# Decode layer on one core: w_up in two loads, w_down in blocks of 4, 4 and 5 rows, and a two-row store of the result

## The chip, the core and the metric

The kernel runs on one NeuronCore of a Trainium2 chip. The metric is the device time of one execution in microseconds (us). "Engines" are PE (matmul), PEld (its weight loads), DVE (vector), ACT (scalar), POOL (GpSimd) and SP (sync), which issues nearly all DMA loads here. "DMA engine" is one of the sixteen that move the bytes (the page counts 16, and a load over 128 partitions has 16 completions in the traces). "Landing" is the time of the last completion that a transfer reports.

## The reference, cut to what matters

One token passes through a pre-norm layer: attention over a cache of 32 heads x 4096 positions x 128, then a gated MLP.

```python
h  = x + attention(layernorm(x), k_cache, v_cache, wq, wo)     # x: 1 x 640
g  = layernorm(h) @ w_gate                                     # 640 x 1728
u  = layernorm(h) @ w_up                                       # 640 x 1728
h2 = h + (gelu(g) * u) @ w_down                                # 1728 x 640
```

All is bf16. The weights and caches are 84 MB and each is read once, so the kernel is a stream of loads with arithmetic beside it. The change concerns the last lines: the loads of w_up and w_down, the products with them, and the store of h2.

## The kernel before: the parts that the change touches

The 640 rows of w_gate and w_up lie as 128 partitions x 5 chunks. Of the 1728 rows of w_down, 13 x 128 form row blocks 0 to 12, and the first 64 rows stand apart in wd_lo (blocks 13 and 14). All loads leave from one queue, in program order.

```python
# loads, in queue order (K, V and wo come earlier)
wd_v = B_w_down[192:1728, :].rearrange("(a p r) n -> p a r n", a=3, r=4)
wd_d = wd_sb[:, 0:12, :].rearrange("p (a r) n -> p a r n", a=3)
d_w1 = P.dma("sync", wd_sb[:, 12, :], B_w_down[64:192, :], mults[NG - 1, 1])
for o in (0, 1, 2, 3, 32, 33, 34, 35):          # 4 partitions each, at a step of 4
    lo = o - o % 32
    d_wp = P.dma("sync", wd_lo[o:o + 13:4, :, :], ..., c_wd, chan="wp")
d_wg = P.dma("sync", wg_sb, B_w_gate[:, :].rearrange("(p c) n -> p c n", c=5), pvs[NG - 2])
d_wu = P.dma("sync", wu_sb, B_w_up[:, :].rearrange("(p c) n -> p c n", c=5))
d_wd = [P.dma("sync", wd_d[:, a, lo:hi, :], wd_v[:, a, lo:hi, :])
         for a, lo, hi in ((0, 0, 4), (1, 0, 4), (2, 0, 3), (2, 3, 4))]
# ... cut: wo products, layer norm ...
def glu(ps, w, *ws):        # 5 chunks x 15 columns of output; w's columns 4 apart for 12 of 15, adjacent for 3
    ...
ga = glu(ps_g, wg_sb, hl, d_wg)
up = glu(ps_u, wu_sb, d_wu)
# ... cut: gelu; g9 multiplies by u and writes hm ...
def down(ms, qs=range(4)):  # a product per row block m and quarter q of the 640 columns
    ...                     # quarter q accumulates in PSUM partition 32 * q, 160 columns
T(down([12]), g9, d_w1)
T(down([13, 14]), d_wp)
T(down(range(4)), d_wd[0])
T(down(range(4, 8)), d_wd[1])
T(down(range(8, 11)), d_wd[2])
dn = {q: T(down([11], [q]), d_wd[3]) for q in (0, 2, 1, 3)}
os = [V(lambda e, q=q: e.tensor_copy(out_row[0:1, 160 * q:160 * q + 160], ps_d[32 * q:32 * q + 1, 0:160]), dn[q])
      for q in range(2)]
os += [A(lambda e, q=q: e.copy(out_row[0:1, 160 * q:160 * q + 160], ps_d[32 * q:32 * q + 1, 0:160]), dn[q])
       for q in range(2, 4)]
d_out = P.dma("sync", out[0, :, :], out_row[:, :], *os)
P.op("sync", None, d_out)
```

`P.dma(engine, out, in, waits...)` issues a transfer; `V`, `A`, `T` put an instruction on DVE, ACT or PE with what it waits for.

The softmax here doesn't subtract the row's maximum and nothing guards it: scores larger than these inputs give would overflow.

## Time and profile before

| | before |
|---|---|
| median time | 202.98 us (202.97 to 203.59, 3 runs) |
| span of the profiled execution | 201.9 us |
| DMA | 84.30 MB, 418 GB/s over the span |
| w_up landed, hm started | 194.62, 197.35 us |
| last w_down load landed | 199.31 us |
| last product ends, store issued | 199.95, 200.69 us |
| store: last completion | 201.82 us |

To read it: the DMA engines are full until about 197 us (81% busy from 197.0 to 197.5, 34% in the half microsecond after it), so the last 5 us are the only place where this change can win. The lines themselves are shown in the prediction below. One line that it only tells of is the page's chain, followed back from the end, by line:

```profile
DMA v_slot<-in_A_v_cache_dram 55%; DMA v_slot<-in_B_w_up_dram 13%; PE psum L363 8%; DVE prod L375 7%; PE psum L167 6%; SPq L59 3%; DVE sc L381 2%; PE psum L492 1%; PE psum L514 1%; PE psum L352 1%; DVE out_row L524 0%; DVE hm L507 0%; DVEq L114 0%
```

The reader is to see w_up's load in second place and no w_down load at all.

### The profile page before, as it was taken

Reading aid. Unit: us, or ns where it says so; the run is one execution under the profiler, and the core shown is the slowest. Engines: PE = TensorE matmul, PEld = TensorE weight load, DVE = VectorE, ACT = ScalarE, POOL = GpSimd, SP = SyncE. Lnnn points to the kernel's source line nnn. Section 1 sums busy time; section 2 is a strip of 40 time slices with the busy share of each in tenths; the row PEclk is TensorE's granted clock in tenths of the full one; section 3 lists DMA queues with packets and bytes.
Section 4 is the critical chain, followed back from the end, with each engine's and each line's share of the span. In section 5 each row is a group of like instructions: output and inputs, shape, how many; then the busy total and the mean of one; then the engine's idle time right before and its main releaser. Section 6 shows DMA issues by size and latency. Waiting matters only on the chain.

```text
span 201.9 us, 2002 instructions
## 1 busy us (share of the span) xinstructions
PE 121.4 (60%) x1008; PEld 34.7 (17%) x756; DVE 100.9 (50%) x51; ACT 12.6 (6%) x33; POOL 30.6 (15%) x36
## 2 busy tenths in 40 slices
PE   0108009849408980994379166934990786779665
PEld 0101000001200120112011101020120012279563
DVE  0110197885598039906960993089519914120321
ACT  2010100001000100010000000100100010100101
POOL 6400000000010007101700450026006300100000
PEclk9999999999955698599579755995797599555555
DMA  9999999999999999999999999999999999999991
GB/s 341 422 425 435 429 422 429 416 474 425 429 422 422 422 448 448 435 416 429 422 422 474 422 429 422 429 416 474 429 429 416 429 422 444 402 419 444 428 387 61
DMA packets 3848, 84.30 MB, mean 418 GB/s; under 512 B 450, under 2 KB 772, under 8 KB 1156
## 3 DMA queue, kind: packets, MB, share of 16 engines
q1 hardware_dynamic: 3842, 84.23, 97.6%
q8 instruction: 4, 0.07, 0.1%
q10 hardware_dynamic: 2, 0.00, 0.0%
HBM read 84.23 MB, written 0.00 MB: 417 GB/s over the span
## 4 chain that ended last, share of the span: by engine, by line
DMA 68%; PE 18%; DVE 10%; SPq 3%; issue 1%; DVEq 0%
DMA v_slot<-in_A_v_cache_dram 55%; DMA v_slot<-in_B_w_up_dram 13%; PE psum L363 8%; DVE prod L375 7%; PE psum L167 6%; SPq L59 3%; DVE sc L381 2%; PE psum L492 1%; PE psum L514 1%; PE psum L352 1%; DVE out_row L524 0%; DVE hm L507 0%; DVEq L114 0%
## 5 line engine op out<-in xcount | busy, mean ns | idle before, releaser
L375 DVE TENSOR_TENSOR prod<-k_slot,qb 128x8192 bf16<-128x8192 bf16 x16 | 75.2, 4734 | 7.0 <-DMA k_slot<-in_A_k_cache_dram 5.2
L167 PE MATMUL psum<-prod,id_b 128*128 128x512 bf16 x233 | 65.4, 437 | 0.0
L381 DVE TENSOR_REDUCE sc<-psum 128x128 f32<-128x2048 f32 x8 | 18.3, 2291 | 49.1 <-PE psum L167 49.1
L352 PE MATMUL psum<-prod,id_b 128*128 128x512 bf16 x23 | 10.7, 467 | 50.5 <-DVE prod L375 47.1
L385 POOL TENSOR_TENSOR p_bd<-pt,own 128x512 bf16<-128x512 bf16 x6 | 24.4, 4071 | 89.5 <-ACT pt L382 89.5
L363 PE MATMUL psum<-v_slot,p_bd 128*16 128x512 bf16 x224 | 18.2, 484 | 5.1 <-DMA v_slot<-in_A_v_cache_dram 5.0
L352 PEld LDWEIGHTS psum<-prod,id_b 128*128 128x128 bf16 x23 | 2.3, 100 | 72.4 <-DVE prod L375 50.4
L369 PEld LDWEIGHTS psum<-hs,po_sb 128*128 128x128 f32 x64 | 9.1, 208 | 23.9 <-issue 23.4
L363 PEld LDWEIGHTS psum<-v_slot,p_bd 128*16 128x16 bf16 x224 | 5.8, 105 | 36.0 <-DMA v_slot<-in_A_v_cache_dram 27.9
L369 PE MATMUL psum<-hs,po_sb 128*128 128x4 f32 x64 | 8.5, 256 | 0.1
L392 ACT COPY po_sb<-psum 128x512 f32<-128x512 f32 x7 | 4.1, 586 | 71.8 <-PE psum L363 71.8
L382 ACT ACTIVATE pt<-sc,zero_t 128x128 bf16<-128x128 f32 x8 | 3.2, 401 | 71.2 <-DVE sc L381 71.2
L335 PE MATMUL psum<-arena,xlnB 128*32 128x512 bf16 x20 | 3.3, 627 | 6.2 <-DMA arena<-in_A_wq_dram 6.2
L462 PE MATMUL psum<-aP,arena 128*128 128x1 bf16 x160 | 6.7, 178 | 0.1
L462 PEld LDWEIGHTS psum<-aP,arena 128*128 128x128 bf16 x160 | 6.6, 131 | 0.2 <-DMA arena<-in_A_wo_dram 0.2
L492 PE MATMUL psum<-hlnT,v_slot 128*128 128x1 bf16 x150 | 5.1, 171 | 1.8 <-DMA v_slot<-in_B_w_up_dram 1.8
L389 POOL MEMSET spare<- 1x1 f32 x1 | 0.1, 90 | 36.6 <-DVE p_bd L385 36.6
L492 PEld LDWEIGHTS psum<-hlnT,v_slot 128*128 128x128 bf16 x150 | 5.0, 116 | 2.4 <-DMA v_slot<-in_B_w_up_dram 1.9
L308 PE MATMUL psum<-one_bf,x_row 1*128 1x1 bf16 x5 | 0.4, 177 | 8.3 <-DMA x_row<-in_A_x_dram 8.3
L363 PE MATMUL psum<-k_slot,p_bd 128*16 128x512 bf16 x32 | 3.6, 629 | 2.9 <-DVE p_bd L385 2.9
L340 DVE CAST qb<-psum 128x512 bf16<-128x512 f32 x1 | 0.7, 692 | 9.1 <-PE psum L167 9.1
L311 DVE COPY xx<-psum 128x5 f32<-128x5 f32 x1 | 0.2, 165 | 8.7 <-PE psum L308 8.7
(72 smaller groups left out, 35.1 us busy)
## 6 DMA issues: line engine op xcount, KB each, us to landing
k_slot<-in_A_k_cache_dram SPq DMA_DIRECT2D x8, 4096.0 KB, 25.5
v_slot<-in_A_v_cache_dram SPq DMA_DIRECT2D x7, 4096.0 KB, 16.7
arena<-in_A_wq_dram SPq DMA_DIRECT2D x1, 5120.0 KB, 15.8
arena<-in_A_wo_dram SPq DMA_DIRECT2D x2, 2560.0 KB, 34.5
k_slot<-in_A_v_cache_dram SPq DMA_DIRECT2D x1, 4096.0 KB, 26.1
v_slot<-in_B_w_gate_dram SPq DMA_DIRECT2D x1, 2160.0 KB, 21.3
v_slot<-in_B_w_up_dram SPq DMA_DIRECT2D x1, 2160.0 KB, 25.9
k_slot<-in_B_w_down_dram SPq DMA_DIRECT2D x2, 640.0 KB, 27.6
```

Of the source, the lines that this page charges most:

```text
L59: ev = self.op(eng, lambda e: e.dma_start(out, in_), *deps, dma=True, chan=chan)
L167: built = e.matmul(out, lhsT, rhs, start=start, stop=stop)
L335: mm = held if hf else lambda e, *a, **k: e.matmul(*a, **k)
L352: mm = held if n or not first else lambda e, *a, **k: e.matmul(*a, **k)
L363: i = e.matmul(ps_o[a:a + 16, :], p_bd[:, 4 * b:4 * b + 4, :].rearrange("p g j -> p (g j)"), vt[:, 4 * b:4 * b + 4, :], start=(b < 4), sto ...
L369: i = e.matmul(ps_a[:, bass.ds(at, 4)], po_sb[:, 128 * r:128 * r + 128], hs[:, r, :], start=(r == 0), stop=(r == 3))
L375: mults[G, i] = VM(lambda e: e.tensor_tensor(out=prod[:, i, :, :], in0=kt[:, 64 * i:64 * i + 64, :], in1=qb[:, G, :].unsqueeze(1).to_broad ...
L381: reds[G] = VR(lambda e: e.reduce_sum(sc[:, :], ps_f.rearrange("p (g d) -> p g d", d=16), axis=AX.X), folds[G, 1])
L385: blocks[G] = on(lambda e: e.tensor_tensor(out=p_bd[:, :, :], in0=pt[:, :].unsqueeze(2).to_broadcast([128, 128, 4]), in1=own[:, :].unsquee ...
L392: evs[G] = AS(lambda e: e.copy(po_sb[:, :], ps_o), pvs[G])
L462: r = e.matmul(ps_p[:, c:c + 1], wo_sb[:, i, c::5], aP[:, i:i + 1], start=False, stop=(i == 31), skip_group_check=True)
L492: i = e.matmul(ps[:, m:m + 1], ws, hlnT[:, c:c + 1], start=(c == 0 and m == 0), stop=(c == 4), skip_group_check=True)
```

## The change

The intent: start the products with w_up before all of it is there, keep the wait for w_down short at the end, and empty PSUM with one copy per engine in place of two. The first takes two loads. The second takes the 160 KB of row block 12 out of the front of the queue. For the third, quarters 0 and 1 of PSUM (partitions 0 and 32) are copied by one DVE instruction over 33 partitions, quarters 2 and 3 by one of ACT. The result then lies in partitions 0 and 32 and is stored as two rows. With the new row blocks, 5 of the 15 weight loads per chunk of w_gate and w_up take columns 5 apart, 8 take columns 4 apart and 2 adjacent ones; before, it was 12 at 4 and 3 adjacent.

```diff
-    out_row = sb("out_row", [1, D], BF16)
+    out_row = sb("out_row", [33, 320], BF16)
...
-    d_w1 = P.dma("sync", wd_sb[:, 12, :], B_w_down[64:192, :], mults[NG - 1, 1])
+    blocks_d = ((64, 0, 4), (576, 4, 4), (1088, 8, 5))
+    def down_load(j, lo, hi):    # rows lo to hi of block j, waits for mults[NG - 1, 1]
...
-    d_wu = P.dma("sync", wu_sb, B_w_up[:, :].rearrange("(p c) n -> p c n", c=5))
-    d_wd = [... for a, lo, hi in ((0, 0, 4), (1, 0, 4), (2, 0, 3), (2, 3, 4))]
+    d_wu = [P.dma("sync", wu_sb[:, lo:hi, :], wu_v[:, lo:hi, :]) for lo, hi in ((0, 3), (3, 5))]
+    d_wd = [down_load(0, 0, 4), down_load(1, 0, 4), down_load(2, 0, 4), down_load(2, 4, 5)]
...
+    col = (0, 320, 160, 480)     # first column of each quarter
...
-    up = glu(ps_u, wu_sb, d_wu)
+    glu(ps_u, wu_sb, range(3), d_wu[0])
+    up = glu(ps_u, wu_sb, range(3, 5), d_wu[1])
...
-    T(down([12]), g9, d_w1)
-    T(down([13, 14]), d_wp)
+    T(down([13, 14]), g9, d_wp)
...
-    T(down(range(8, 11)), d_wd[2])
-    dn = {q: T(down([11], [q]), d_wd[3]) for q in (0, 2, 1, 3)}
-    os = [ ... four copies of 1 x 160 ... ]
-    d_out = P.dma("sync", out[0, :, :], out_row[:, :], *os)
+    T(down(range(8, 12)), d_wd[2])
+    dn = [T(down([12], [q]), d_wd[3]) for q in range(4)]
+    os = [V(lambda e: e.tensor_copy(out_row[0:33, 0:160], ps_d[0:33, 0:160]), dn[1]),
+          A(lambda e: e.copy(out_row[0:33, 160:320], ps_d[64:97, 0:160]), dn[3])]
+    d_out = P.dma("sync", out[0, :, :].rearrange("o (q n) -> (o q) n", q=2), out_row[::32, :], *os)
```

(Cuts are marked with "...".)

More of the change, by code (lines that the diff above doesn't have):

```diff
@@ L443, in bass_sequential_preLN__gqa_block_cached__glu_gated_geglu__decode_kernel @@
     wd_sb = k_slot[1][:, 0:15 * D].rearrange("p (m n) -> p m n", m=15)
-    wd_v = B_w_down[192:1728, :].rearrange("(a p r) n -> p a r n", a=3, r=4)
-    wd_d = wd_sb[:, 0:12, :].rearrange("p (a r) n -> p a r n", a=3)
-    d_w1 = P.dma("sync", wd_sb[:, 12, :], B_w_down[64:192, :], mults[NG - 1, 1])
+    blocks_d = ((64, 0, 4), (576, 4, 4), (1088, 8, 5))
+    at_row = {m0 + r: (lo + r, k) for lo, m0, k in blocks_d for r in range(k)}
+    def down_load(j, lo, hi):
+        row, m0, k = blocks_d[j]
+        return P.dma("sync", wd_sb[:, m0 + lo:m0 + hi, :],
+                     B_w_down[row:row + 128 * k, :].rearrange("(p r) n -> p r n", r=k)[:, lo:hi, :], mults[NG - 1, 1])
     for o in (0, 1, 2, 3, 32, 33, 34, 35):
@@ L451, in bass_sequential_preLN__gqa_block_cached__glu_gated_geglu__decode_kernel @@
     d_wg = P.dma("sync", wg_sb, B_w_gate[:, :].rearrange("(p c) n -> p c n", c=5), pvs[NG - 2])
-    d_wu = P.dma("sync", wu_sb, B_w_up[:, :].rearrange("(p c) n -> p c n", c=5))
-    d_wd = [P.dma("sync", wd_d[:, a, lo:hi, :], wd_v[:, a, lo:hi, :])
-             for a, lo, hi in ((0, 0, 4), (1, 0, 4), (2, 0, 3), (2, 3, 4))]
+    wu_v = B_w_up[:, :].rearrange("(p c) n -> p c n", c=5)
+    d_wu = [P.dma("sync", wu_sb[:, lo:hi, :], wu_v[:, lo:hi, :]) for lo, hi in ((0, 3), (3, 5))]
+    d_wd = [down_load(0, 0, 4), down_load(1, 0, 4), down_load(2, 0, 4), down_load(2, 4, 5)]
     T(lambda e: e.matmul(ps_p[:, 0:5], id_f[:, :], xx[:, 0:5], start=True, stop=False, skip_group_check=True), xc, c_idf)
@@ L471, in resid @@
             i = e.matmul(ps_d[32 * q:32 * q + 1, 0:160], ones_f[:, 0:1],
-                         hX[:, 32 * q:32 * q + 32, :].rearrange("p a c -> p (a c)"), start=True, stop=False)
+                         hX[:, col[q] // 5:col[q] // 5 + 32, :].rearrange("p a c -> p (a c)"), start=True, stop=False)
         return i
@@ L479, in bass_sequential_preLN__gqa_block_cached__glu_gated_geglu__decode_kernel, with glu @@
         hlnT[:, :], hT[:, 0:5], ln[:, 0:1], ln[:, 4:5], ALU.subtract, ALU.mult), residual)
-    def glu(ps, w, *ws):
+    def glu(ps, w, cs, *deps):
         def fn(e):
-            for c in range(5):
+            for c in cs:
                 for m in range(15):
-                    if m < 12:
-                        ws = w[:, c, 192 + 512 * (m // 4) + m % 4:192 + 512 * (m // 4) + 512:4]
-                    elif m == 12:
-                        ws = w[:, c, 64:192]
+                    if m < 13:
+                        lo, k = at_row[m]
+                        ws = w[:, c, lo:lo + 127 * k + 1:k]
                     else:
@@ L494, in fn @@
             return i
-        return T(fn, *ws)
-    ga = glu(ps_g, wg_sb, hl, d_wg)
-    up = glu(ps_u, wu_sb, d_wu)
+        return T(fn, *deps)
+    ga = glu(ps_g, wg_sb, range(5), hl, d_wg)
+    glu(ps_u, wu_sb, range(3), d_wu[0])
+    up = glu(ps_u, wu_sb, range(3, 5), d_wu[1])
     g1 = V(lambda e: e.tensor_tensor(out=g_t[:, :], in0=ps_g[:, 0:15], in1=own_g[:, :], op=ALU.mult), ga, c_gm)
@@ L514, in fn @@
                     i = e.matmul(ps_d[32 * q:32 * q + 1, 0:160], hm[0:rows, m:m + 1],
-                                 wd[0:rows, 160 * q:160 * q + 160], start=False, stop=(m == 11))
+                                 wd[0:rows, col[q]:col[q] + 160], start=False, stop=(m == 12))
             return i
         return fn
-    T(down([12]), g9, d_w1)
-    T(down([13, 14]), d_wp)
+    T(down([13, 14]), g9, d_wp)
     T(down(range(4)), d_wd[0])
     T(down(range(4, 8)), d_wd[1])
-    T(down(range(8, 11)), d_wd[2])
-    dn = {q: T(down([11], [q]), d_wd[3]) for q in (0, 2, 1, 3)}
-    os = [V(lambda e, q=q: e.tensor_copy(out_row[0:1, 160 * q:160 * q + 160], ps_d[32 * q:32 * q + 1, 0:160]), dn[q])
-          for q in range(2)]
-    os += [A(lambda e, q=q: e.copy(out_row[0:1, 160 * q:160 * q + 160], ps_d[32 * q:32 * q + 1, 0:160]), dn[q])
-           for q in range(2, 4)]
-    d_out = P.dma("sync", out[0, :, :], out_row[:, :], *os)
+    T(down(range(8, 12)), d_wd[2])
[3 more added lines that the diff above has]
+    d_out = P.dma("sync", out[0, :, :].rearrange("o (q n) -> (o q) n", q=2), out_row[::32, :], *os)
     P.op("sync", None, d_out)
```

## The prediction

> **What bounds the kernel now.** I read the page first (whole span), then the DMA issues, the timeline of the last 20 us, the chain of waits, and last a table of half-microsecond windows over the end. The page's second part shows that nothing but the transfers can bound the bulk of the kernel:
>
> ```profile
> PE   0108009849408980994379166934990786779665
> DMA  9999999999999999999999999999999999999991
> GB/s 341 422 425 435 429 422 429 416 474 425 429 422 422 422 448 448 435 416 429 422 422 474 422 429 422 429 416 474 429 429 416 429 422 444 402 419 444 428 387 61
> ```
>
> The DMA row is 9 in 39 of 40 slices of 5.05 us, and 84.30 MB move at about 420 GB/s. The change moves the same weight bytes, so up to the last slice it can only reorder transfers. What is left to win lies after 191 us, and there these lines of the timeline carry the argument (columns: start, duration, engine, line, operation, count, idle time before it and what ended it):
>
> ```profile
> 187.35 0.17 DVE L468 COPY hT<-psum 128x5 f32<-128x5 f32 x1 [6.93 <-PE psum L462]
> 190.27 2.57 PE L492 MATMUL psum<-hlnT,v_slot 128*128 128x1 bf16 x75
> 194.67 2.58 PE L492 MATMUL psum<-hlnT,v_slot 128*128 128x1 bf16 x75 [1.83 <-DMA v_slot<-in_B_w_up_dram]
> 197.35 0.17 DVE L507 TENSOR_TENSOR hm<-gu,psum 128x15 bf16<-128x15 f32 x1 [2.84 <-PE psum L492]
> 197.58 0.30 PE L514 MATMUL psum<-k_slot,hm 128*1 128x160 bf16 x4 [0.33 <-DVE hm L507]
> 197.81 0.43 PE L514 MATMUL psum<-wd_lo,hm 48*1 48x160 bf16 x8
> 198.18 1.77 PE L514 MATMUL psum<-k_slot,hm 128*1 128x160 bf16 x48
> 199.97 0.66 DVE L524 CAST out_row<-psum 1x160 bf16<-1x160 f32 x2 [2.45 <-PE psum L514]
> 200.01 0.60 ACT L526 CAST out_row<-psum 1x160 bf16<-1x160 f32 x2 [6.20 <-PE psum L514]
> 200.69 0.27 SPq L59 DMA_DIRECT2D out_dram<-out_row  x1
> ```
>
> The reader is to see one serial tail: w_up has landed at 194.62, its 75 products take 2.58 us, hm follows, then 60 products with w_down (4 + 8 + 48), two copies one after the other on each engine, and the store. The chain of waits names the same: w_up's transfer, then L492, L507, L514, L524. Read alone, it promises about 1.5 us for splitting w_up. But the chain shows only the waits that ended last. The next one is hidden just behind it, in the issues of w_down (KB, microseconds from issue to landing, taken in windows around each issue):
>
> ```profile
> 169.15 0.43 SPq L59 DMA_DIRECT2D k_slot<-in_B_w_down_dram  x1
> k_slot<-in_B_w_down_dram SPq DMA_DIRECT2D x1, 640.0 KB, 27.0
> ...
> 169.62 1.59 SPq L59 DMA_DIRECT2D k_slot<-in_B_w_down_dram  x1
> k_slot<-in_B_w_down_dram SPq DMA_DIRECT2D x1, 640.0 KB, 28.1
> ...
> k_slot<-in_B_w_down_dram SPq DMA_DIRECT2D x1, 480.0 KB, 27.7
> k_slot<-in_B_w_down_dram SPq DMA_DIRECT2D x1, 160.0 KB, 27.6
> ```
>
> The four big loads land at 169.15 + 27.0 = 196.2, 169.62 + 28.1 = 197.7, 171.25 + 27.7 = 198.95 and 171.7 + 27.6 = 199.3 us (the third issue begins where the second ends, 169.62 + 1.59 + 0.04; the view of w_down's tile gives 171.7 as the last issue's start). The products of 198.18 to 199.95 never wait, because each block is there a few tenths before its turn. **So w_down's last landing, 199.3, lies only 0.65 us before the end of the last product.** That is the floor under any gain ahead of the products.
>
> [...] the last w_down load's 16 completions spread from 197.28 to 199.31. [...] weight loads of the w_down products come in groups of four every 133 ns. [...] within a row of 15, start to start is 33 ns where the columns are 4 apart, 27 ns where they are adjacent, and 40 ns in the wo products (5 apart). [...]
>
> **The change, part by part.**
>
> 1. *The 160 KB load of row block 12 leaves the front of the queue and becomes part of blocks 0 to 12.* Everything that follows it up to w_up lands earlier by 160 KB / 420 GB/s = 0.39 us: w_gate about 189.1, w_up about 194.2. The gate gains nothing, since it starts at 190.27 on hlnT. The blocks land at 195.8, 197.35, 198.95 (block 2, now 4 rows of 160 KB and not 3) and 199.3: the last two don't move, because the bytes ahead of them are the same.
>
> 2. *The eight small loads no longer stand behind the wait for the last k_slot use.* They can be issued near 147 us and w_gate and w_up after them, and not at 162 to 169. The queue is full in either case (w_gate lay 21.3 us and w_up 25.9 us in it), and the order within it stays. Worth 0.
>
> 3. *w_up in 3 and 2 of its 5 chunks.* The second part is 864 KB, 2.1 us of queue, so the first lands near 192.1, before the gate is through.
>
> 4. *Columns 5 apart.* Per chunk the loads go from 12 x 33.3 + 3 x 27 = 481 ns to 8 x 33.3 + 5 x 40 + 2 x 27 = 520 ns, so +0.04 us a chunk, +0.2 us for the gate and +0.2 for up. Gate 190.27 to 193.05; up's first part to about 194.7 (3 x 0.52 and a little), second part, already there since 194.2, to 195.75. hm, which stood at 197.35, starts near 195.8: **1.5 us earlier**.
>
> 5. *The products with w_down.* Rows 13 and 14 at 196.05, 0.45 us; rows 0 to 3 at once; rows 4 to 7 wait for 197.35; rows 8 to 11 wait for 198.95. From there 16 + 4 products are left, five groups of four. The old run of 48 took 1.77 us = 12 x 0.133 + 0.17, so five take 5 x 0.133 + 0.17 = 0.84 us. With 0.05 us from landing to start the last one ends at 199.83, where it ended at 199.95. Of the 1.5 us, **0.12 us** arrives; the rest turns into a new wait for w_down of about 0.8 us before rows 8 to 11, and a shorter one before rows 4 to 7.
>
> 6. *The copies.* One per engine and not two in a row. Thirty-three partitions cost what one does[...]: 0.30 to 0.32 us and not 0.60 to 0.66. They now wait for the second and the fourth product of the last row; these four end within some 20 ns, so nothing is lost. **Worth 0.33 us**, all of it on the path.
>
> 7. *The store.* Still 1,280 B, in two rows of 640 B from partitions 0 and 32. From issue to the end of the wait it took 1.1 us (200.69 to 201.82, by the trace's completion) and is latency, not bytes. Worth 0; at worst +0.1.
>
> Sum: 0.12 + 0.33 = 0.45 us, less a doubt of 0.05 to 0.1 for the two-row store and the semaphores. I take 0.4: **202.98 - 0.4 = 202.6 us**.
>
> **Rivals.**
>
> *A: w_up was the bound, and all 1.5 us arrives, with the copies 1.8 us: 201.2.* For it speaks the chain, which names w_up. Against it the landings: no product may end before 199.3 plus one group and its drain, and 195.8 to 199.3 has only 1.9 us of product work in it. It could come true only if the queue itself ended a microsecond earlier. Fewer packets (128 of 1,280 B gone, 128 added by the split of w_up) don't do that.
>
> *B: the slowest engine shifts.* The landing that counts is that of one engine in sixteen; the next stands at 198.83, half a microsecond earlier. [...]
>
> *C: a new cost takes more than it saves.* Candidates are a slow 33-partition copy (0.3 us each[...]), a slower two-row store, and the weight loads 5 apart. The last is hidden by the wait for w_down, 0.4 us against 1.5. All others together give about 203.2.
>
> *D: earlier issues choke the queue or change the order.* The issue of the last w_down row was held 7.6 us (171.7 to 179.3) in the queue already and did no harm, since its bytes were needed at 199. With the small loads queued earlier the hold may move to an earlier block, with some 16 us of slack.
>
> **Range and chances.** All parts of the change that can reach the end sum to under 2 us, and 2% is 4.06 us. So only something outside this argument, such as a hole in the transfers of 4 us, makes it leave the band. The old kernel's own three runs spread over 0.6 us (202.97 to 203.59), and rival B is worth half a microsecond either way: low 202.0, high 203.2. Chances: faster by over 2% 0.01, within 0.98, slower 0.01.
>
> **What would show it.** In the changed kernel's profile: up's products in two runs of 45 and 30 that wait for nothing but the gate (point 3); hm near 195.8 (4); idle time of the matmul engine on w_down's transfer, 0.5 to 1.2 us, which the old profile hasn't got (5); one copy on each of the two engines of about 0.3 us (6); the store issued near 200.3 and not 200.69 (sum). The prediction is wrong if w_down's last landing moves by more than 0.5 us, if the matmul engine doesn't wait for w_down, or if the copy of 33 partitions takes twice that of one.

The sum is 0.12 + 0.33 = 0.45 us less 0.05, so 0.4 us and 202.6. The 0.33 us took it as given that a copy of 33 partitions costs what one of a single partition does. The prediction had no measurement for that; the changed profile has (317 ns beside 314). The times from one weight load to the next (33, 27 and 40 ns) and the groups of four every 133 ns are read from the trace of the kernel before. Rival B's bounds were 202.1 and 203.1, the 0.5 us between the two latest completions (198.83 and 199.31) to either side of 202.6; that instruction fetches could cause such a shift was not shown. An estimate that the experiments come back to: 0.78 us of extra work on four DMA engines, 20 KB on each, at a sixteenth of 420 GB/s. That four carry each of the eight small loads is read from the trace of the kernel before: of their 40 completions 8 come while they are issued, and 32, four a load, from 182.41 to 183.97.

## The result, and the profile after

| | before | after |
|---|---|---|
| median time | 203.0 us (202.97 to 203.59, 6 runs) | 203.04 us (202.99 to 203.11, 6 runs) |
| span of the profiled execution | 201.9 us | 201.8 us |
| hm started | 197.35 | 196.41 |
| last w_down load landed | 199.31 | 199.16 |
| last product ends | 199.95 | 199.67 |
| store issued | 200.69 | 200.12 |
| store: last completion | 201.82 | 201.72 |

The ratio of times is 0.9997, with a 95% interval of 0.9984 to 1.001: the same. Ratios here are the mean time of one kernel's fast runs over that of the other's fast runs of the same rounds, so they aren't quite the ratio of the medians in the tables.

The timeline of the changed kernel's end (start, duration, engine, line, operation, count, idle time before it and what ended it):

```profile
190.10 5.12 PE L495 MATMUL psum<-hlnT,v_slot 128*128 128x1 bf16 x144
195.94 0.37 PE L495 MATMUL psum<-hlnT,v_slot 128*128 128x1 bf16 x6 [0.71 <-issue]
196.41 0.17 DVE L510 TENSOR_TENSOR hm<-gu,psum 128x15 bf16<-128x15 f32 x1 [1.88 <-PE psum L495]
196.64 0.43 PE L517 MATMUL psum<-wd_lo,hm 48*1 48x160 bf16 x8 [0.33 <-DVE hm L510]
197.00 1.23 PE L517 MATMUL psum<-k_slot,hm 128*1 128x160 bf16 x32
198.83 0.84 PE L517 MATMUL psum<-k_slot,hm 128*1 128x160 bf16 x20 [0.59 <-DMA k_slot<-in_B_w_down_dram]
199.70 0.32 DVE L526 CAST out_row<-psum 33x160 bf16<-33x160 f32 x1 [3.12 <-PE psum L517]
199.75 0.29 ACT L527 CAST out_row<-psum 33x160 bf16<-33x160 f32 x1 [5.91 <-PE psum L517]
200.12 0.58 SPq L59 DMA_DIRECT2D out_dram<-out_row  x1
```

The gate and up now run through 144 products without a stop, 6 follow after a gap of 0.71 us, and hm comes 0.94 us earlier. But the 20 products of 198.83 have waited 0.59 us for w_down, a wait that the old profile hasn't got. The copies are one per engine. The last line is the surprise: issuing the store lasted 0.58 us and not 0.27. The chain of the same profile, by line, now names w_down in w_up's place:

```profile
DMA v_slot<-in_A_v_cache_dram 71%; DMA k_slot<-in_B_w_down_dram 14%; PE psum L363 9%; SPq L59 4%; PE psum L517 0%; ACT out_row L527 0%
```

The view of the result's tile shows the copies and the store alone (duration in ns as min/median/max). Of the kernel before:

```profile
L524 DVE CAST out_row<-psum x2: 312/314/316, 200.0 to 200.3; 1x160 bf16<-1x160 f32 x2
L526 ACT CAST out_row<-psum x2: 285/286/287, 200.0 to 200.3; 1x160 bf16<-1x160 f32 x2
L59 SPq DMA_DIRECT2D out_dram<-out_row x1: 272/272/272, 200.7 to 200.7; - x1
```

Of the changed one:

```profile
L526 DVE CAST out_row<-psum x1: 317/317/317, 199.7 to 199.7; 33x160 bf16<-33x160 f32 x1
L527 ACT CAST out_row<-psum x1: 289/289/289, 199.7 to 199.7; 33x160 bf16<-33x160 f32 x1
L59 SPq DMA_DIRECT2D out_dram<-out_row x1: 577/577/577, 200.1 to 200.1; - x1
```

A copy of 33 partitions takes 317 ns where one of a single partition took 314, so the copies did what they were meant to. The store's issue takes 577 ns where it took 272. Counted to the last completion, the store went from 201.82 - 200.69 = 1.13 us to 201.72 - 200.12 = 1.60 us.

So the sum over the end of the kernel reads: products end 0.28 us earlier (of which 0.15 because all loads of this execution happened to land that much earlier), copies 0.74 - 0.45 = 0.29 us less, the store 0.47 us more. Together 0.10 us less, as the two last completions say (201.82 and 201.72). Without the 0.15 us that belong to the execution it is 0.05 us more. Both are less than the medians can tell.

### The profile page after: what moved, and what is told of

Same layout as the page of the kernel before. It is cut to its first block, busy times and chain, and to the rows that moved or that the text cites. A ratio compares the mean times of both kernels' runs of the same rounds, so it can differ in the third digit from the quotient of the medians.

```text
span 201.8 us, 2001 instructions
## 1 busy us (share of the span) xinstructions
PE 119.7 (59%) x1009; PEld 33.6 (17%) x756; DVE 100.4 (50%) x50; ACT 12.3 (6%) x32; POOL 30.8 (15%) x36
## 4 chain that ended last, share of the span: by engine, by line
DMA 85%; PE 9%; SPq 4%; issue 0%; ACT 0%
DMA v_slot<-in_A_v_cache_dram 71%; DMA k_slot<-in_B_w_down_dram 14%; PE psum L363 9%; SPq L59 4%; PE psum L517 0%; ACT out_row L527 0%
## 5 line engine op out<-in xcount | busy, mean ns | idle before, releaser
L167 PE MATMUL psum<-prod,id_b 128*128 128x512 bf16 x233 | 64.8, 433 | 0.0
L352 PE MATMUL psum<-prod,id_b 128*128 128x512 bf16 x23 | 10.5, 456 | 50.6 <-DVE prod L375 47.4
L369 PEld LDWEIGHTS psum<-hs,po_sb 128*128 128x128 f32 x64 | 8.3, 191 | 24.1 <-issue 23.5
L369 PE MATMUL psum<-hs,po_sb 128*128 128x4 f32 x64 | 7.7, 244 | 0.4 <-ACT po_sb L428 0.4
```

Source lines behind the costliest of these rows:

```text
L167: built = e.matmul(out, lhsT, rhs, start=start, stop=stop)
L352: mm = held if n or not first else lambda e, *a, **k: e.matmul(*a, **k)
L369: i = e.matmul(ps_a[:, bass.ds(at, 4)], po_sb[:, 128 * r:128 * r + 128], hs[:, r, :], start=(r == 0), stop=(r == 3))
```

## The experiments

Two theories stood against each other. **The store theory**: the products and copies won their 0.3 to 0.45 us as planned, and the two-row store gave it back. **The rival**: the gain was never there (the split of w_up or the new blocks cost elsewhere, and the long store belongs to one execution). And one question came with it: what makes the two-row store slow? Every experiment was timed in five rounds against the kernel before and profiled once, and no run was over 1.5% above the fastest of its kernel. The runs fall into sets of rounds on different chips (the four about the store; w_up in one load, the last block, the finer loads and the small loads over 16 engines; the three others), so across sets the ratio to before is the safer comparison. By the 2% rule every one of them is "same"; what follows is about tenths of a microsecond.

| run | median us (range, 6 runs) | ratio to before (95%) |
|---|---|---|
| changed kernel | 203.04 (202.99 to 203.11) | 0.9997 (0.9984 to 1.001) |
| changed kernel again | 202.92 (202.82 to 203.16) | 0.9989 (0.9975 to 1.0002) |
| one-row store put back | 202.93 (202.83 to 203.1) | 0.999 (0.9977 to 1.0003) |
| before, with the new store only | 203.05 (202.97 to 203.12) | 0.9994 (0.9981 to 1.0006) |
| two one-row stores, two queues | 202.58 (202.45 to 202.65) | 0.9972 (0.996 to 0.9985) |
| rows from adjacent partitions (wrong result) | 202.48 (202.39 to 202.66) | 0.9967 (0.9954 to 0.998) |
| w_up in one load | 202.81 (202.78 to 203.03) | 0.9984 (0.9968 to 1.0) |
| last w_down block not loaded (wrong result) | 202.24 (201.75 to 202.71) | 0.9956 (0.9938 to 0.9975) |
| two queues, last block in 2, 2, 1 rows | 202.54 (202.43 to 202.61) | 0.9966 (0.995 to 0.9982) |
| small loads over 16 engines | 203.95 (203.82 to 204.02) | 1.0036 (1.002 to 1.0052) |
| two queues, w_up in one load | 202.55 (202.48 to 202.6) | 0.9969 (0.9956 to 0.9982) |
| small loads into adjacent partitions | 203.16 (202.93 to 203.29) | 0.9999 (0.9985 to 1.0013) |

### The old store in the changed kernel

```diff
-    os = [ ... one 33-partition copy on DVE, one on ACT ... ]
-    d_out = P.dma("sync", out[0, :, :].rearrange("o (q n) -> (o q) n", q=2), out_row[::32, :], *os)
+    os = [ ... two copies of 1 x 160 on DVE, two on ACT, into partition 0 ... ]
+    d_out = P.dma("sync", out[0, :, :], out_row[:, :], *os)
```

> The changed kernel with only the old end put back: two copies in a row on each engine into one partition, one row of 1280 B stored. Theory (the two-row store gave back what the copies and products had won): from the issue of the store to the last completion 1.13 us instead of 1.60, from the end of the products to the issue 0.7 instead of 0.45; last product still at about 199.7. So about 0.15 us faster than the changed kernel, 202.85. Rival (the lost gain went elsewhere, before the store): 203.3, slower by the 0.3 us of the copies.

Measured: 202.93 us, 0.1 us under the changed kernel and not above it. In its profile the copies take 0.66 us again, the store's issue 0.27 us, and from issue to last completion 200.33 to 201.46 = 1.13 us. Undoing the new copies and the new store at once loses nothing, so the two cancel. The rival, which had the loss before the store, is out by 0.4 us. The issue, in this run's timeline:

```profile
200.33 0.27 SPq L59 DMA_DIRECT2D out_dram<-out_row  x1
```

### The new store in the kernel before

```diff
 kernel before, with:
+    out_row = sb("out_row", [33, 320], BF16)
+    col = (0, 320, 160, 480)     # and its use in the residual, the products, the copies
+    os = [ ... one 33-partition copy on DVE, one on ACT ... ]
+    d_out = P.dma("sync", out[0, :, :].rearrange("o (q n) -> (o q) n", q=2), out_row[::32, :], *os)
```

> The kernel before with only the end of the change: one 33-partition copy per engine and the two-row store. Theory: copies win 0.33, the two-row store loses 0.47, so 0.1 to 0.15 us slower than before, and the store's issue lasts 0.58 and not 0.27. Rival (the longer store belongs to that profiled run or to the other parts of the change): 0.3 us faster than before.

Measured: 203.05 us beside 203.03 for the kernel before in the same rounds. The store's issue took 578 ns, and 200.15 to 201.75 = 1.60 us passed to its last completion:

```profile
200.15 0.58 SPq L59 DMA_DIRECT2D out_dram<-out_row  x1
```

The profile repeats the 0.47 us to the hundredth, and so do the others with this store: 1.59 to 1.60 us in all seven profiles; the 0.1 us by which the whole should be slower is below what the runs resolve. The rival's 0.3 us gain isn't there.

### Two rows, two queues

```diff
-    d_out = P.dma("sync", out[0, :, :].rearrange("o (q n) -> (o q) n", q=2), out_row[::32, :], *os)
-    P.op("sync", None, d_out)
+    d_out = [P.dma("sync", out[0, :, 0:320], out_row[0:1, :], *os),
+             P.dma("scalar", out[0, :, 320:640], out_row[32:33, :], *os)]
+    P.op("sync", None, *d_out)
```

> The changed kernel, with its store split in two one-row stores, one issued by the sync engine and one by the scalar engine. Theory (the slow part is one transfer over two rows): each issue lasts 0.27 us, the store takes 1.1 us again, and the kernel is 0.4 us faster than the changed one, 202.6. Rival (two rows or two small writes are slow however they are issued): within 0.1 us of 203.0.

Measured: 202.58 us, 0.46 us under the changed kernel (0.34 us under its second measurement, below), as the store theory said. The view of the result's tile in this run:

```profile
L59 ACTq DMA_DIRECT2D out_dram<-out_row x1: 228/228/228, 199.9 to 199.9; - x1
L59 SPq DMA_DIRECT2D out_dram<-out_row x1: 272/272/272, 199.9 to 199.9; - x1
```

The two issues stand side by side and each is short. From the first issue to the last completion 199.91 to 201.17 = 1.26 us pass. The same two rows, of the same size, aren't slow in themselves. This is also **the version that beats both kernels**: its interval, 0.996 to 0.9985, lies wholly under 1, and its slowest run (202.65) is under the fastest of the changed kernel's twelve (202.82). It is 0.3% and not 2%.

### Two rows from adjacent partitions

```diff
-    d_out = P.dma("sync", ..., out_row[::32, :], *os)
+    d_out = P.dma("sync", ..., out_row[0:2, :], *os)
```

The second half of the result is wrong; only the step between the partitions changes.

> The changed kernel with the two rows taken from partitions 0 and 1 and not 0 and 32 (half of the result is wrong on purpose). If the step of 32 partitions makes the issue slow: issue 0.27 us and 202.6. If two rows over two engines do, whatever the step: issue 0.58 us and 203.0.

Measured: 202.48 us. One line of its profile decides it, from the view of the result's tile:

```profile
L59 SPq DMA_DIRECT2D out_dram<-out_row x1: 280/280/280, 200.1 to 200.1; - x1
```

One transfer, two rows, and the issue takes 280 ns and not 577; to the last completion 200.11 to 201.24 = 1.13 us pass, as with one row. So it is **the step of 32 partitions in the access pattern** that costs 0.3 us of issue and 0.47 us in all, not the number of rows or of bytes. Nor is it partition 32 itself: with two queues the row from there was issued in 228 ns. How the issue is worked through inside, no run shows. The packets in the traces place the delay: the store's first packet starts 0.75 us after the issue begins in the kernel before and here, and 1.22 us after it in the changed kernel; from that packet to the last completion 0.38 to 0.39 us pass in all three. So the whole 0.47 us pass before a byte moves, 0.30 in the issue and 0.17 between its end and the first packet.

### w_up in one load

```diff
-    d_wu = [... for lo, hi in ((0, 3), (3, 5))]
-    glu(ps_u, wu_sb, range(3), d_wu[0])
-    up = glu(ps_u, wu_sb, range(3, 5), d_wu[1])
+    d_wu = [... for lo, hi in ((0, 5),)]
+    up = glu(ps_u, wu_sb, range(5), d_wu[0])
```

> The changed kernel with w_up loaded whole again. Theory (w_down's landing sets the end of the products, and the early start of up is eaten by the wait for it): hm 0.5 to 1 us later than in the changed kernel, the wait before rows 8 to 11 shorter or gone, the last product still within 0.1 us of 199.7, time within 0.1 us of 203.04. Rival (the split of w_up is worth the 1.5 us that the chain of waits gave it): 0.5 us slower or more.

Measured: 202.81 us, if anything faster than the changed kernel. The details of the theory missed: hm came 0.32 us later and not 0.5 to 1, the last product ended 0.3 us earlier and not within 0.1, partly because all of this execution's loads landed some 0.2 us earlier (the second wo load at 183.53 against 183.75). In its timeline:

```profile
193.86 2.76 PE L495 MATMUL psum<-hlnT,v_slot 128*128 128x1 bf16 x75 [1.22 <-DMA v_slot<-in_B_w_up_dram]
197.32 2.05 PE L516 MATMUL psum<-k_slot,hm 128*1 128x160 bf16 x52
198.53 0.49 PEld L516 LDWEIGHTS psum<-k_slot,hm 128*1 128x1 bf16 x20 [0.32 <-DMA k_slot<-in_B_w_down_dram]
```

Up waits 1.22 us for w_up again, the products start at 196.96 in place of 196.64, and yet they end at 199.37. The weight loads of the last 20 still wait 0.32 us for w_down. So even with w_up whole, w_down is there last, and what the chain of the kernel before put down to w_up is worth next to nothing with this order of loads. The 0.2 us by which this run seems faster shrank when both forms were run again (below).

### The last block of w_down not loaded

```diff
-    d_wd = [down_load(0, 0, 4), down_load(1, 0, 4), down_load(2, 0, 4), down_load(2, 4, 5)]
+    d_wd = [down_load(0, 0, 4), down_load(1, 0, 4)]
-    rows, wd = (128, wd_sb[:, m]) if m < 13 else ...
+    rows, wd = (128, wd_sb[:, m % 8]) if m < 13 else ...
```

Products 8 to 12 read rows that are there already, so the result is wrong.

> The changed kernel without the last two w_down loads (800 KB less; the products of rows 8 to 12 read rows 0 to 4, so the result is wrong on purpose). It takes away the landing that the products wait for. Theory: 60 products run without a stop from hm and end near 198.9, 0.75 us earlier, time 202.3; the transfers end 1.9 us earlier, yet only 0.75 of it arrives. Rival (the transfers set the end directly): 1.9 us earlier. Rival (the products are the bound already): no change.

Measured: 202.24 us, 0.8 us under the changed kernel; the six runs spread over 1 us, more than any other kernel's. The timeline shows the products running through:

```profile
196.04 0.43 PE L517 MATMUL psum<-wd_lo,hm 48*1 48x160 bf16 x8 [0.34 <-DVE hm L510]
196.40 2.01 PE L517 MATMUL psum<-k_slot,hm 128*1 128x160 bf16 x52
198.45 0.32 DVE L526 CAST out_row<-psum 33x160 bf16<-33x160 f32 x1 [2.46 <-PE psum L517]
```

Without that landing the last product ends at 198.41, 1.26 us before the changed kernel's. Here 0.6 us of it is an hm that came earlier in this execution (195.81 against 196.41: the gate began 0.19 us earlier and the gap before its last six products was 0.43 us shorter). The rest, 0.66 us, is about the wait for w_down that the changed kernel has (0.59). The profiled execution was the fastest of the six (201.75 us). The transfers themselves end 2.2 us sooner (197.00 against 199.16), which does not arrive. Both rivals are out.

### Finer loads at the end

```diff
 two queues, and
-    down_load(2, 0, 4), down_load(2, 4, 5)]
+    down_load(2, 0, 2), down_load(2, 2, 4), down_load(2, 4, 5)]
```

> The two one-row stores of the earlier run, and the last w_down block in loads of 2, 2 and 1 rows, so that the landing at about 198.8 has two rows of products behind it and not four. Theory: five groups of products after that landing become one after the landing at 199.1: the last product near 199.35 and not 199.67, 0.3 us off; with the stores 202.25. Rival (one more load moves the last landing later by as much): 202.6.

Measured: 202.54 us, against 202.58 with two queues alone. A miss: I expected 0.3 us. Its timeline has two waits in place of one:

```profile
198.92 0.70 PE L517 MATMUL psum<-k_slot,hm 128*1 128x160 bf16 x12 [0.32 <-DMA k_slot<-in_B_w_down_dram]
199.31 0.09 PEld L517 LDWEIGHTS psum<-k_slot,hm 128*1 128x1 bf16 x4 [0.29 <-DMA k_slot<-in_B_w_down_dram]
```

The last four products do start alone, right after the last landing, but that landing is at 199.27 here and was at 198.96 with two queues. To take the execution's own shift out, I count from the landing of the second wo load to w_down's last. That stretch is 15.36 us in the two runs with the new blocks and w_up whole, 15.41 to 15.45 in the six with w_up in two loads, and 15.46 with the finer loads. That would be about 0.05 us of queue for a load more, but the kernel before has as many loads in the stretch as the changed one, and took 15.40 and, with the new store, 15.35; so it isn't shown. At most it explains a sixth of the miss. The whole stream also came later here (the second wo load landed at 183.81 against 183.55), which a single profile can't separate from chance. Counted from that landing, the last product ends at 15.80 us here and at 15.91 with two queues alone: a gain of 0.1 us and not 0.3, which the medians don't show.

### The small loads over all engines

```diff
-    for o in (0, 1, 2, 3, 32, 33, 34, 35):   # 4 partitions each, at a step of 4
-        ...
+    for lo in (0, 32):
+        d_wp = P.dma("sync", wd_lo[lo:lo + 16, :, :],
+                     B_w_down[lo:lo + 32, :].rearrange("(r p) n -> p r n", r=2), c_wd, chan="wp")
```

> The changed kernel with the eight loads of 4 partitions into wd_lo made two loads of 16 partitions, so that all engines carry them. If the four engines that carry them now are the late ones, as the prediction took it: the last landing 0.5 us earlier and the kernel 0.5 us faster, 202.5. If they are engines that run ahead (the completions of the wo load before them spread over 2.2 us already): the last landing 0 to 0.2 us later, 203.1.

Measured: 203.95 us, 0.9 us slower. Both expectations missed, the first in sign and the second in size. The second wo load landed at 184.29 (183.75 in the changed kernel) and the stretch from there to w_down's last landing took 15.74 us (15.41). The four engines with extra work were not the late ones: in the changed kernel the 16 completions of the second wo load spread over 2.0 us (181.73 to 183.75), and those of the small loads, whose work comes after it, run from 182.07 to 183.81, so the last is level with the slowest of the wo load. So, by these completions, the old arrangement gives the extra bytes to engines that are ahead. That the spread loads lose because late engines now get a share fits this, but sixteen engines writing into sixteen neighbouring partitions is a second candidate, and no run parts the two.

### The small loads into adjacent partitions

```diff
-        d_wp = P.dma("sync", wd_lo[o:o + 13:4, :, :], ...)      # partitions o, o+4, o+8, o+12
+        d_wp = P.dma("sync", wd_lo[lo:lo + 4, :, :], ...)       # partitions lo to lo+3
```

> The changed kernel with the eight small loads still over four engines each, but into 4 adjacent partitions and not 4 partitions at a step of 4. [...] If the run with the loads spread over 16 engines lost 0.9 us because late engines got work too, this one stays at 203.0. If it lost it because the loads wrote into neighbouring partitions at the same time, this one is slower too, by some tenths. In either case the issue of each load should take 0.3 to 0.45 us and not 0.62, if a step between partitions is what makes an issue slow.

Measured: 203.16 us, 0.12 and 0.24 us above the two measurements of the changed kernel, so loads into four neighbouring partitions lose little or nothing of the 0.9 us; sixteen weren't tried apart. The view of the tile gives what this run was also for, the length of the eight issues. The changed kernel:

```profile
L59 SPq DMA_DIRECT2D wd_lo<-in_B_w_down_dram x8: 618/622/821, 147.9 to 152.7; - x8
```

This run:

```profile
L59 SPq DMA_DIRECT2D wd_lo<-in_B_w_down_dram x8: 257/299/377, 146.3 to 148.8; - x8
```

The same bytes over as many partitions, and the issue takes 299 ns with adjacent partitions and 622 with a step of 4. It is the store's finding on a load, with another step; but here the rows on the DRAM side changed with it, from a step of four rows to adjacent ones, and no run parts the two sides. The shorter issues win no time: the loads land some 35 us after they are issued, behind a full queue.

### The changed kernel again, and two queues with w_up whole

The first has no edit. The second takes the two-queue store and the one-load w_up together.

> The changed kernel once more, unaltered, beside the next run on one chip: 203.0 by every theory; it shows what of the 0.2 us that the kernel with w_up in one load was faster is more than a difference of rounds.

> The two one-row stores and w_up in one load together. If both gains are real and add (0.46 and 0.2): 202.4. If the 0.2 was a difference of rounds: 202.6. The last completion of w_down follows that of the second wo load by 15.35 us (15.41 with w_up in two loads).

Measured: 202.92 and 202.55 us. The changed kernel moved by 0.12 us from one set of rounds to the next, and two queues gained nothing more from w_up in one load (202.55 against 202.58). So the 0.2 us above was mostly a difference of rounds. The split of w_up neither helps nor hurts by more than the medians can tell.

The profiles tell more when the execution's shift is taken out. Counted from the landing of the second wo load, the store's last completion comes at:

| | us |
|---|---|
| kernel before | 17.91 |
| before, with the new store | 18.03 |
| changed kernel, twice | 17.97, 17.98 |
| one-row store put back | 17.84 |
| w_up in one load | 17.89 |
| two queues | 17.62 |
| adjacent rows | 17.51 |
| two queues, w_up in one load | 17.54 |
| two queues, finer loads | 17.51 |
| small loads into adjacent partitions | 18.00 |
| small loads over 16 engines | 18.25 |
| last w_down block not loaded | 16.91 |

These are single executions, but the changed kernel repeats to 0.01 us, and the store theory's small differences, which the medians couldn't show, stand here: the new store alone costs 0.12 us (0.1 to 0.15 expected), the old one put back wins 0.13 (0.15 expected). The split of w_up costs 0.08 us in both pairs.

## Why the prediction was right or wrong

The forecast of "the same" and the range held: 203.04 lies in 202.0 to 203.2. The centre was 0.4 us low, and the predicted gain did not come. That the range held is owed to the room it left for the rivals and not to the sum: B, a shift of the slowest engine, didn't come about (w_down's last landing followed the second wo load's by 15.40 us before and 15.41 after), and a candidate of C did. None of the three signs that were to show the prediction wrong appeared either: none of them watched the length of the store. Term by term:

- **Points 1 and 3, the landings**, came as computed: 188.87 for w_gate, 191.97 and 194.09 for w_up, 195.63, 197.22, 198.79 and 199.16 for w_down, each 0.1 to 0.25 us before the forecast, of which 0.15 is the execution's.
- **The floor** ("w_down's last landing ... is the floor under any gain ahead of the products") held. The landing moved by 0.15 us with the execution, the matmul engine waited 0.59 us for w_down where it hadn't before, and taking the landing away freed the products. What it waited for, as point 5 has it, was the landing of rows 8 to 11 at 198.79, and the last landing came while their products ran. Rival A, all 1.5 us of the chain, was rightly refused, though its "1.9 us of product work" was too small: from 197.58 to 199.95 the same 60 products took 2.37.
- **Point 4, hm 1.5 us earlier**, was 0.94 us. The step priced the gate and up as one run without a break. Its 0.2 us for the columns 5 apart was right: the gate's 75 products take 2.76 us with w_up in one load, and took 2.57 before. But the profile has 0.71 us of idle time before the last six products, ended by nothing that it can name. Such a gap stands at the same six products in all profiled runs whose up was split, 0.28 to 0.78 us long; it was hidden under the wait for w_down. In these nine traces a 16 KB packet of the instruction queue ends 1.38 to 1.62 us before the six products start, while that start wanders over 1.1 us (0.5 us if counted from the gate's start), so a wait for instructions fits; no run tests it, and the cause stays open.
- **Point 2** took the start of w_gate's and w_up's issues for near 147 us. They began at 164.35, because w_gate waits for v_slot to be free and that use ended then. As the point said, it is worth nothing, for the queue was full.
- **Point 5, 0.12 us from the products**, is borne out in the profiles: 0.28 us with a landing 0.15 us earlier, and, counted from the second wo load, 16.03 us (15.98 with the new store) before and 15.91 to 15.95 with the changed loads. The 0.1 us in the medians of the changed kernel with the old store is within the noise.
- **Point 6, 0.33 us from the copies**, measured 0.29 us, the 33 partitions costing what one does (317 ns beside 314).
- **Point 7 is the step that failed**: "Worth 0; at worst +0.1". The store measured +0.47 us. I had reasoned that a store of 1,280 B is latency and that two rows don't change it. In the trace of the kernel before its one packet takes 0.05 of the 1.13 us, and for two rows from neighbouring partitions it is 1.13 us too. With a step of 32 it is 1.60 us, with an issue twice as long (577 ns and not 272). The sum was 0.12 + 0.33 - 0.05; with the store's true size it is 0.12 + 0.33 - 0.47 = -0.02, no gain, as measured (203.04 against 203.0).

The trace of the kernel before held the warning: eight issues of 10 KB over 4 partitions at a step of 4 took 0.62 us each, and w_gate's over 128 adjacent partitions 0.43. I saw the length of those issues and asked only whether it delayed the stream.

Rival C had the right kind ("a slower two-row store") among its candidates, with too small a weight. Rival D's hold did move to an earlier block (the second w_down issue lasted 5.34 us, from 166.16) and did no harm, as the prediction said. The 0.78 us of extra work on four DMA engines was an estimate (80 KB over four engines at a sixteenth of 420 GB/s), and it was no fault to mend: spreading that work cost 0.9 us.

## What to carry to other kernels

At the end of a kernel, where a store stands alone, price its issue from an issue of the same access pattern and not from its bytes: look in the trace for how long issues with a step between partitions take beside those over adjacent ones (here 577 ns beside 280 for the store). For rows that had to lie apart, two single-row stores from two queues were the cheaper form here: 1.26 us to the last completion and not 1.60. And before a wait named by the chain is attacked, list the landings of everything that is still to come: the next one may lie close behind it, as w_down's did here (199.31, 0.65 us before the end of the products). Where the stream of loads shifts from one execution to the next, count from a landing that the change can't move: differences of 0.1 us that the medians hid stood out that way.
